# Per-row scales for whole blocks of q, and a longer planned landing for the transposed weights

## The chip, the cores and the metric

The kernel runs on one core of one Trainium2 chip. The metric is device time in microseconds of one execution, from the median of several runs. The engines are named as in the profile: PE (matmuls; PEld is its weight loads), DVE (the vector engine), ACT (the scalar engine), POOL (GpSimd) and SP (which issues the DMAs).

## What is computed

```python
B, H, S, D = 4, 8, 576, 64
scores = np.matmul(q, k.transpose(0, 1, 3, 2)) / np.sqrt(D)
kth = np.partition(scores, -32, axis=-1)[..., -32:-31]
scores = np.where(scores >= kth, scores, -1e9)
attn = np.exp(scores - scores.max(-1, keepdims=True))
attn = attn / (attn.sum(-1, keepdims=True) + 1e-9)
o = np.matmul(attn, v)
x = o.transpose(0, 2, 1, 3).reshape(B * S, H * D)
h = np.maximum(x @ w_in, 0.0)
x = h * h @ w_out
h = x @ w_in2
return (h * np.clip(h + 3.0, 0.0, 6.0) / 6.0) @ w_out2
```

Attention keeps the 32 largest scores of each row. Two layers follow, 512 to 2048 to 512 features each, over 2304 tokens.

## The kernel before

Every operand of a large matmul is split into two 16-bit parts, a high part and the rest, so that three 16-bit products stand for one 32-bit product. Before the split an operand is multiplied by a power of two, which `scale_pair` (lines 255 to 263) makes on DVE with three small operations from the exponent of a size: the scale for the operand, and its inverse for later.

A batch has 576 tokens: four blocks of 128 (whole blocks) and one of 64 (a tail). Order: 20 blocks over four batches, and in each block tiles of one head (a tail: two heads at once), 144 tiles in all. For q of a block, `q_prep` works in two halves of four heads: a load, `norm_tasks`, the split, and a DMA transpose into `qT`. `norm_tasks` (line 587) lets ACT square the operand with a running sum into `ss`, one number per partition; PE multiplies `ss` with a matrix of ones, which sums over the partitions and puts the total on each (`pnq`, line 599, in a PSUM bank of the pool `misc`); and DVE's `scale_pair` (lines 261 to 263) reads it there. For q a partition is a token, in a tail block a token too.

A tile goes through `attend`: PE multiplies q and k (`qk`, line 764, into `sp`); ACT copies the scores to S (line 770, three buffers); DVE finds the 32 largest in seven operations (lines 778 to 786) and masks the exponentials (line 801); POOL and ACT make the bias and the exponentials (lines 790, 795); ACT and POOL split the weights into `wc` (lines 806, 810, 811); SP issues a DMA transpose of `wc` into `wT` (`flip`, line 815, two buffers), and PE multiplies with the values (`av`, line 829, 14 matmuls, or 28 in a tail). When a block's tiles are through, `x_operand` makes the input of the layers (`pnx`, line 916). The layers run in groups of matmuls: `up` into `hb` (line 1075), ACT and in the second layer a gate on DVE (line 1090), a split into `ghl` on ACT and POOL, and `acc` (lines 1110 and 1118). Their scales use another `pnx` (line 1000).

The order of all instructions is made when the kernel is built. Each step is a `task` with an engine, a planned cost, a key and the tasks it needs; `Plan.run` plays a list scheduler over the engines. A task becomes ready for those that need it at its planned end plus a latency `lat`, by default one per engine (`LAT`, for SP 2.0 us). An engine takes, among its ready tasks, the one with the smallest key whose buffers are free. So PE's tasks have keys 1 for `qk`, 2 for `av`, 4 for `acc` and 5 for `up`: an `av` that is ready goes before any matmul of the layers. What comes out is one fixed list for each engine, and on the chip each engine works through its list in order and waits where an input is not there yet. The flip's task has a cost of 1.25 and the default latency:

```python
LAT = {"ACT": 0.17, "DVE": 0.14, "POOL": 0.12, "PE": 0.21, "SP": 2.0}
tw = task("SP", 1.25, (0, s), flip, deps=[tl, before[4]], alloc=["wT"])
tv = task("PE", 0.44 if len(hs) == 1 else 0.9, (2, s), av, deps=[tw, vv_task[b, hp][1], before[5]],
          alloc=["av"] if t == 0 else [])
```

Of the kernel before, what the change touches and what calls it, by code (L numbers as in the profile page):

```python
# [19 lines left out]
P = 128  # L20
# [5 lines left out]
EXP_I = float(50 << 23)  # L26
# [6 lines left out]
class Plan:  # L33
# [11 lines left out]
    def task(self, eng, cost, key, fn, deps=(), alloc=(), reads=(), writes=(), lat=None, port=False):  # L45
        t = Task(eng, cost, key, fn, tuple(alloc), lat or LAT[eng])
        t.port = port
        need = {d for d in deps if d is not None}
        for r in reads:
            need.add(self.writer.get(r))  # L50
            self.readers.setdefault(r, []).append(t)
        for r in writes:
            need.add(self.writer.get(r))
            need.update(self.readers.pop(r, ()))
            self.writer[r] = t
        need -= {None, t}
        t.left = len(need)
        for d in need:
            d.succ.append(t)
        self.tasks.append(t)  # L60
        return t

    def free(self, name, owner, *users):
        e = [len(users), name, owner]
        for u in users:
            u.rel.append(e)
# [66 lines left out]
def tile_topk_attention_moe_moe2(  # L133
# [52 lines left out]
    task, free = plan.task, plan.free  # L186
# [13 lines left out]
    def take(name, label=None):  # L200
        if name == "stg":
            return stg[plan.current.slot[name]]
        if isinstance(size[name], int):
            c = size[name] + plan.current.slot.get(name, 0)
            return scalars[:, c:c + 1]
        shape, dtype, where = size[name]
        return where.tile(shape, dtype, tag=f"{name}{plan.current.slot[name]}", name=label or name, bufs=1)
# [49 lines left out]
    def scale_pair(y_ap, inv, add, sc):  # L257

        e = scalars[:, size["e"] + nexp[0] % 4:size["e"] + nexp[0] % 4 + 1].bitcast(I32)
        nexp[0] += 1  # L260
        nc.vector.tensor_scalar(e, y_ap.bitcast(I32), EXPMASK, 1, op0=ALU.bitwise_and, op1=ALU.logical_shift_right)
        nc.vector.tensor_scalar(sc.bitcast(I32), e, -1.0, EXP_S, op0=ALU.mult, op1=ALU.add)
        nc.vector.tensor_scalar(inv.bitcast(I32), e, 1.0, add, op0=ALU.mult, op1=ALU.add)
# [49 lines left out]
    def kb(space, lo, hi):  # L313

        return [(space, n_) for n_ in range(int(lo), -int(-hi // 1))]
# [51 lines left out]
    def w_convert(i, n_, pn, par):  # L367
# [3 lines left out]
        src = kb(PLACE[i][n_][0], 4 * PLACE[i][n_][1], 4 * PLACE[i][n_][1] + 4) if PLACE[i][n_] and is64 else []  # L371
        key = CKEY[i][0] + CKEY[i][1] * n_
        low = is64 and n_ % 4 < NPOOL[i] and (i < 3 or n_ < 9)
# [210 lines left out]
    def when(kkey):  # L584
        return first[kkey[1]] + 2.0 * kkey[2] if kkey[0] == "q" else first[first_of(order, kkey[1])] + kkey[2]

    def norm_tasks(tag, src, junk, n, cost, deps, alloc, inv, kkey, reads=(), writes=()):

        box = {}

        def square():
            for a_ in alloc:
                T[a_, kkey] = take(a_)
            box["ss"] = take("ss")
            nc.scalar.activation(junk(), src(), AF.Square, accum_out=box["ss"][0:n])

        def total():
            box["pn"] = take("misc", "pn" + tag)
            nc.tensor.matmul(box["pn"][:, 0:1], ones32[0:n, :], box["ss"][0:n], start=True, stop=True)

        def scale():
            box["sc"] = take("sc" + tag)
            scale_pair(box["pn"][:, 0:1], inv(), EXP_I, box["sc"])

        t1 = task("ACT", cost, (PREP, when(kkey)), square, deps=deps, alloc=["ss", *alloc], reads=reads, writes=writes)
        t2 = task("PE", 0.2, (0, when(kkey)), total, deps=[t1], alloc=["misc"])
        t3 = task("DVE", 0.34, (0, when(kkey)), scale, deps=[t2],
                  alloc=["sc" + tag] + (["qinv"] if tag == "q" else []))
        free("ss", t1, t2)
        free("misc", t2, t3)  # L610
        return box, t1, t3

    def kv_prep(which, b, hp, deps):
# [33 lines left out]
        if which == 0:  # L647
# [5 lines left out]
            def kn5():  # L653
                return kn().rearrange("p (h c a d) -> p h c a d", h=2, c=NCH, a=2)

            bx, t1, t3 = norm_tasks("k", lambda: box["f"].rearrange("p h c d -> p (h c d)"),
                                    lambda: kn().bitcast(BF16)[:, 0:n_], P, 0.72, [l1, l2], alloc, lambda: inv, kkey,
                                    reads=rd, writes=kbn if b == 0 else [])
# [13 lines left out]
        else:  # L672
            def vv():
                return T["vv", kkey]

            bx, t1, t3 = norm_tasks("v", lambda: box["f"].rearrange("p h c d -> p (h c d)"),
                                    lambda: vv().rearrange("p a h c d -> p (a h c d)").bitcast(BF16)[:, 0:n_],
                                    P, 0.72, [l1, l2], ["vv"], lambda: inv, kkey, reads=rd)
# [8 lines left out]
    def q_prep(i, half):  # L687
# [21 lines left out]
        def qn():  # L709
            return T["kn", kkey][:, 0:16 * D].rearrange("p (h a c d) -> p h a c d", h=4, a=2, c=2)  # L710

        bx, t1, t3 = norm_tasks("q", lambda: box["f"][0:n].rearrange("p h d -> p (h d)"),
                                lambda: T["kn", kkey][0:n].bitcast(BF16)[:, 0:4 * D], n, 0.4, [l], ["kn", "qT"],
                                lambda: T.setdefault(("qinv", kkey), None) or T.__setitem__(("qinv", kkey), take("qinv"))
# [36 lines left out]
    def attend(s):  # L751
# [80 lines left out]
        before = tile_tasks[-1] if tile_tasks else [None] * 6  # L832
# [6 lines left out]
        for r in range(7):  # L839
            prev = task("DVE", 0.73 if r % 2 else 0.667, (2, s + 0.1 * r), lambda r=r: topk(r), deps=[prev],  # L840
                        alloc=["m"] if r == 0 else ["W"] if r == 1 else [])
# [7 lines left out]
                  alloc=["sums"] if t == 0 else [])  # L849
# [3 lines left out]
        th = task("ACT", 0.57, (AKEY[2], s), high, deps=[tm, before[2]], alloc=["wc"])  # L853
        tl = task("POOL", 1.38, (AKEY[3], s), low, deps=[th, before[3]])
        free("E", te, tl)
        tw = task("SP", 1.25, (0, s), flip, deps=[tl, before[4]], alloc=["wT"])
        free("wc", th, tw)
        tv = task("PE", 0.44 if len(hs) == 1 else 0.9, (2, s), av, deps=[tw, vv_task[b, hp][1], before[5]],
                  alloc=["av"] if t == 0 else [])
# [372 lines left out]
    for i, (b, j) in enumerate(order):  # L1232
        if i == first_of(order, b) and b:
            for hp in range(NHP):
                for which in range(2):
                    kv_prep(which, b, hp, late)
        if i:
            for half in range(2):
                q_prep(i, half)
        for s in range(first[i], last[i] + 1):  # L1240
            attend(s)
        x_operand(i)
# [13 lines left out]
def first_of(order, b):  # L1256
    return min(i for i, e in enumerate(order) if e[0] == b)
# [25 lines left out]
PREP = 1.5  # L1283
VKEY = 3

CKEY = ((-3.61, 0.14), (-69.99, 3.36), (-31.64, 0.91), (-0.36, 1.29))
SKEY = (0, 100, 200, 300)

# [26 lines left out]
```

## Time and profile before

| | |
|---|---|
| median of 3 runs | 1236.63 us (1236.08 to 1240.48) |
| the profiled execution's own time | 1238.58 us |
| its span, first to last instruction | 1236.8 us |
| PE, PEld, DVE busy | 1074.3, 879.4, 1058.9 us |
| ACT, POOL busy | 825.4, 663.8 us |
[...]

The durations below all come from the profiled execution. Busy shares are means over the whole span; the stretches differ, and a stretch has to be read for itself. A busy PE need not be a PE at its peak, since matmuls overlap in the records and their ends are modelled: the step from one to the next is shorter than the time of one.

### The profile page before, as it was taken

What the parts mean: (1) busy time and instruction counts of PE and PEld (TensorE: products, weight loads), DVE (VectorE), ACT (ScalarE), POOL (GpSimd) and SP (SyncE); (2) the same over time, 40 slices, a digit from 0 to 9 for tenths busy, and PEclk for the clock granted to TensorE, in tenths of its full rate; (3) what the DMA queues carried; (4) which work ended last, traced back from release to release, by engine and by line L of the source; (5) the groups of instructions that cost most, each with busy time, mean ns of one, the idle gap of its engine ahead of it and who ended that gap; (6) DMA issues with size and microseconds to landing.
All of it is one profiled execution on the core that took longest, in us unless ns stands there. A gap on an engine that the chain in (4) does not pass through costs nothing.

```text
span 1236.8 us, 36708 instructions
## 1 busy us (share of the span) xinstructions
PE 1074.3 (87%) x14856; PEld 879.4 (71%) x14856; DVE 1058.9 (86%) x2463; ACT 825.4 (67%) x1580; POOL 663.8 (54%) x969
## 2 busy tenths in 40 slices
PE   2484389878989999999899999999998999999998
PEld 2332147577679769877887888788767868978885
DVE  5999999999978999999999999999868989999011
ACT  7677588769767668666766757576866666755422
POOL 5857846458654556554545555655544555545312
PEclk9676599998999999999899999999998999999999
DMA  9989744333454233344574323435433233433100
GB/s 209 268 247 265 228 101 115 71 55 55 96 113 93 53 63 70 66 71 82 89 109 72 68 56 71 55 64 98 97 59 73 54 66 73 65 49 58 22 2 18
DMA packets 276762, 112.47 MB, mean 91 GB/s; under 512 B 257521, under 2 KB 265713, under 8 KB 276593
## 3 DMA queue, kind: packets, MB, share of 16 engines
q1 hardware_dynamic: 276592, 110.14, 43.3%
q8 instruction: 116, 1.90, 0.6%
q14 instruction: 54, 0.43, 0.1%
HBM read 48.23 MB, written 4.72 MB: 43 GB/s over the span
## 4 chain that ended last, share of the span: by engine, by line
PE 42%; DVE 15%; ACT 10%; DMA 10%; issue 5%; POOL 5%; SPq 1%; POOLq 0%; DVEq 0%; ACTq 0%
PE hb L1075 16%; PE acc L1118 9%; PE acc L1110 8%; DMA wT<-wc 8%; DVE W L783 4%; DVE m L786 4%; PE av L829 3%; PE sp L764 3%; DVE E L801 2%; DVE m L778 2%; POOL wc L810 1%; ACT E L795 1%; POOL ghl L1100 1%; ACT x L896 1%; ACT S L770 1%
## 5 line engine op out<-in xcount | busy, mean ns | idle before, releaser
L1075 PE MATMUL hb<-hl,w 128*128 128x128 f16 x6912 | 455.8, 220 | 3.7 <-ACT r L1082 2.2
L1075 PEld LDWEIGHTS <-w 128*128 128x128 f16 x6912 | 415.7, 99 | 42.8 <-issue 6.2
L786 DVE MAX8 m<-W 128x8 f32<-128x576 f32 x432 | 314.8, 747 | 0.2
L1100 POOL TENSOR_TENSOR ghl<-r,ghl 128x512 f16<-128x512 f32 x144 | 172.7, 1201 | 193.3 <-ACT ghl L1097 141.9
L1110 PE MATMUL acc<-ghl,w 128*128 128x128 f16 x3456 | 242.0, 221 | 9.9 <-POOL ghl L1100 4.2
L810 POOL TENSOR_TENSOR wc<-E,wc 128x512 f16<-128x512 f32 x144 | 167.8, 1165 | 145.2 <-ACT wc L806 117.8
L1118 PE MATMUL acc<-w,ghl 128*128 128x512 f16 x864 | 234.3, 382 | 2.8 <-POOL ghl L1100 1.5
L1110 PEld LDWEIGHTS <-w 128*128 128x128 f16 x3456 | 212.8, 99 | 29.8 <-issue 14.0
L783 DVE MATCH_REPLACE8 W<-m,W 128x576 f32<-128x576 f32 x288 | 213.3, 742 | 0.0
L795 ACT ACTIVATE E<-S,scalars,scl 128x576 f32<-128x576 f32 x144 | 124.8, 867 | 85.9 <-POOL scalars L790 65.3
L801 DVE SCALAR_TENSOR_TENSOR E<-S,m,E 128x576 f32<-128x576 f32 x144 | 137.2, 952 | 0.1
L770 ACT ACTIVATE S<-sp 128x576 f32<-128x576 f32 x144 | 92.9, 645 | 53.8 <-DVE E L801 40.9
L764 PE MATMUL sp<-kT,qT 128*128 128x288 f16 (+1 forms) x640 | 102.4, 303 | 25.0 <-ACT S L770 21.0
L829 PE MATMUL av<-vv,wT 128*128 128x64 f16 (+1 forms) x2240 | 92.7, 197 | 33.7 <-DMA wT<-wc 32.8
L829 PEld LDWEIGHTS <-wT 128*128 128x128 f16 (+1 forms) x2240 | 81.2, 103 | 56.5 <-DMA wT<-wc 46.9
L1097 ACT ACTIVATE ghl<-r 128x512 f16<-128x512 f32 x144 | 89.8, 626 | 40.9 <-PE acc L1110 21.2
L778 DVE MAX8 m<-S 128x8 f32<-128x576 f32 x144 | 107.3, 746 | 4.9 <-ACT S L770 4.9
L783 DVE MATCH_REPLACE8 W<-m,S 128x576 f32<-128x576 f32 x144 | 106.8, 741 | 0.0
L1118 PEld LDWEIGHTS <-ghl 128*128 128x128 f16 x864 | 73.8, 99 | 45.2 <-issue 3.3
L806 ACT ACTIVATE wc<-E 128x576 f16<-128x576 f32 x144 | 97.7, 679 | 4.6 <-DVE E L801 4.5
L412 POOL TENSOR_TENSOR w<-w,stg 128x512 int32<-128x512 int32 x57 | 73.0, 1294 | 35.4 <-DVE w L365 23.6
L1090 DVE SCALAR_TENSOR_TENSOR r<-r,hb 128x512 f32<-128x512 f32 x72 | 48.9, 680 | 49.6 <-ACT r L1084 49.4
(128 smaller groups left out, 1343.2 us busy)
## 6 DMA issues: line engine op xcount, KB each, us to landing
w<-in_moe_w_in_dram SPq DMA_DIRECT2D x32, 512.0 KB, 4.8
w<-in_moe_w_out_dram SPq DMA_DIRECT2D x29, 512.0 KB, 4.8
out_dram<-o SPq DMA_DIRECT2D x16, 256.0 KB, 2.4
qf<-in_q_dram SPq DMA_DIRECT2D x31, 128.0 KB, 3.1
stg<-in_k_dram SPq DMA_DIRECT2D x12, 256.0 KB, 3.2
stg<-in_v_dram SPq DMA_DIRECT2D x12, 256.0 KB, 3.1
wT<-wc SPq DMA_TRANSPOSE x144, 3.2
stg<-in_moe_w_out_dram SPq DMA_DIRECT2D x6, 256.0 KB, 3.9
```

The lines of the kernel that those rows point to most:

```text
L764: nc.tensor.matmul(dst, qT[:, 2 * ((2 * hp + hh) % 4) + a, 0:M], kflat[:, hh * SPAD + c * HALF:hh * SPAD + (c + 1) * HALF], start=a == 0, ...
L778: nc.vector.max(m[:, 0:8], T["S", s])
L783: nc.vector.match_replace(out=T["W", s], in_to_replace=m[:, 8 * c - 8:8 * c], in_values=T["S", s] if c == 1 else T["W", s], imm_value=-3.0e38)
L786: nc.vector.max(m[:, 4 * r:4 * r + 8], T["W", s])
L795: nc.scalar.activation(T["E", s], T["S", s], AF.Exp, bias=T["nb", s], scale=T["scl", ("q", i, half)][:, hp % 2:hp % 2 + 1])
L801: nc.vector.scalar_tensor_tensor(T["E", s], T["S", s], T["m", s][:, TOPK - 1:TOPK], T["E", s], op0=ALU.is_ge, op1=ALU.mult, accum_out=T["s ...
L810: nc.gpsimd.tensor_tensor(wc[:, S + TAIL:], e[:, 0:S - TAIL], wc[:, 0:S - TAIL], op=ALU.subtract)
L829: nc.tensor.matmul(out_[cols, t * D:(t + 1) * D], wT[0:kr, a, cols], vv[0:kr, vb, hh, c, :], start=n_ == 0, stop=n_ == len(prods) - 1)
L1075: nc.tensor.matmul(box["h"][:, fi * n:(fi + 1) * n], wt[2 * m][:, kk * 4 + f // 4, a, f % 4 * P:(f % 4 + 1) * P], hl[:, c, kk, 0:n], start ...
L1100: nc.gpsimd.tensor_tensor(flat(box["g"][:, 1]), flat(box["r"]), flat(box["g"][:, 0]), op=ALU.subtract)
L1110: nc.tensor.matmul(flat_[:, c * w_:c * w_ + n], wt[1][:, f, a, c * P:(c + 1) * P], gl[d], start=(f, a, d) == (0, 0, 0) and c * w_ % 512 == ...
L1118: nc.tensor.matmul(o_, gl[d][:, ch * P:ch * P + rows], wt[3][:, f, a, :], start=f == 0 and (a, d) == (0, 0), stop=f == KF - 1 and (a, d) = ...
```

## The change

Two edits. In `norm_tasks`, a q half of a whole block (`n == P`) has no sum over partitions: DVE's `scale_pair` reads `ss` itself, so each token has its own power of two, and the inverse that goes into the scores' scale differs by token as well. The task `total` on PE and its bank of `misc` fall away there; `ss` is held until DVE has read it. Tails of q, and k and v, stay as they were. In `attend`, the flip's task gets a latency of its own, `WLAT = 4.0`, in place of 2.0. That adds and removes no instruction; the planner lets `av` become ready 2.0 us later, and so gives all engines another order.

```diff
@@ -600,14 +600,17 @@
 
         def scale():
             box["sc"] = take("sc" + tag)
-            scale_pair(box["pn"][:, 0:1], inv(), EXP_I, box["sc"])
+            scale_pair(box["ss"] if rows else box["pn"][:, 0:1], inv(), EXP_I, box["sc"])
 
         t1 = task("ACT", cost, (PREP, when(kkey)), square, deps=deps, alloc=["ss", *alloc], reads=reads, writes=writes)
-        t2 = task("PE", 0.2, (0, when(kkey)), total, deps=[t1], alloc=["misc"])
+
+        rows = tag == "q" and n == P
+        t2 = t1 if rows else task("PE", 0.2, (0, when(kkey)), total, deps=[t1], alloc=["misc"])
         t3 = task("DVE", 0.34, (0, when(kkey)), scale, deps=[t2],
                   alloc=["sc" + tag] + (["qinv"] if tag == "q" else []))
-        free("ss", t1, t2)
-        free("misc", t2, t3)
+        free("ss", t1, t3 if rows else t2)
+        if not rows:
+            free("misc", t2, t3)
         return box, t1, t3
 
     def kv_prep(which, b, hp, deps):
@@ -853,7 +856,7 @@
         th = task("ACT", 0.57, (AKEY[2], s), high, deps=[tm, before[2]], alloc=["wc"])
         tl = task("POOL", 1.38, (AKEY[3], s), low, deps=[th, before[3]])
         free("E", te, tl)
-        tw = task("SP", 1.25, (0, s), flip, deps=[tl, before[4]], alloc=["wT"])
+        tw = task("SP", 1.25, (0, s), flip, deps=[tl, before[4]], alloc=["wT"], lat=WLAT)
         free("wc", th, tw)
         tv = task("PE", 0.44 if len(hs) == 1 else 0.9, (2, s), av, deps=[tw, vv_task[b, hp][1], before[5]],
                   alloc=["av"] if t == 0 else [])
@@ -1283,6 +1286,8 @@
 PREP = 1.5
 VKEY = 3
 
+WLAT = 4.0
+
 CKEY = ((-3.61, 0.14), (-69.99, 3.36), (-31.64, 0.91), (-0.36, 1.29))
 SKEY = (0, 100, 200, 300)
 
```

What moves, at two places. Line numbers after the change are larger by 3 from `scale` on. First DVE, at one half of q of a whole block of the third batch, after 76 masks. The three operations of `scale_pair` are L261 to L263, MAX and MATCH_REPLACE belong to the search for the 32 largest, and the row that writes `E,sums` is a mask. Before:

```order
L783 MATCH_REPLACE W<-m,S 128x576
L786 MAX m<-W 128x8
L261 TENSOR_SCALAR scalars<-pnq 128x1
L262 TENSOR_SCALAR scalars<-scalars 128x1
L263 TENSOR_SCALAR scalars<-scalars 128x1
L801 SCALAR_TENSOR_TENSOR E,sums<-S,m,E 128x576
L786 MAX m<-W 128x8
```

And in the changed kernel:

```order
L781 MAX m<-S 128x8
L789 MAX m<-W 128x8
L261 TENSOR_SCALAR scalars<-scalars 128x1
L262 TENSOR_SCALAR scalars<-scalars 128x1
L263 TENSOR_SCALAR scalars<-scalars 128x1
L804 SCALAR_TENSOR_TENSOR E,sums<-S,m,E 128x576
L786 MATCH_REPLACE W<-m,S 128x576
```

The three operations stand after the same number of masks; the first reads `scalars` (where `ss` lies) in place of `pnq`.

Second PE, at the 104th tile, the last of a whole block in the third batch. The first row is the last matmul of the `qk` four tiles on, the last row the first matmul of this tile's `av`; the row of `sp` above it ends the `qk` five tiles on. `ghl` and `hl` rows are the layers', pnk is the sum of a k. Before, between the two `qk` stand three matmuls of L1118, the pnk and 60 of L1075:

```order
L764 MATMUL sp<-kT,qT 64x288
L1118 LDWEIGHTS ghl
...
L599 MATMUL pnk<-scalars,ones_75 128x1
L1075 LDWEIGHTS w_88
...
L764 MATMUL sp<-kT,qT 64x288
L829 LDWEIGHTS wT
L829 MATMUL av<-vv,wT 128x64
```

And in the changed kernel (L1121 is the old L1118, L1113 the old L1110, L1078 the old L1075, L832 the old L829), where between the two `qk` stand 9 matmuls of L1121, 48 of L1113, 36 of L1078 and the `av` of the tile before:

```order
L767 MATMUL sp<-kT,qT 64x288
L1121 LDWEIGHTS ghl
...
L1113 LDWEIGHTS w_87
...
L1078 LDWEIGHTS w_88
...
L767 MATMUL sp<-kT,qT 64x288
L599 MATMUL pnq<-scalars,ones_75 128x1
L832 LDWEIGHTS wT
L832 MATMUL av<-vv,wT 128x64
```

The `av` of this tile has moved behind more work of the layers. After the last `av` of the program, PE's list has 612 matmuls of `hb`, 288 of L1110 and 108 of L1118, against 636, 288 and 114 before.

## Rows read from the trace of the kernel before

**Rows 1.** The page, part 1: busy time, share of the span, instructions.

```profile
PE 1074.3 (87%) x14856; PEld 879.4 (71%) x14856; DVE 1058.9 (86%) x2463; ACT 825.4 (67%) x1580; POOL 663.8 (54%) x969
```

**Rows 2.** Busy time of four stretches, clock, DMA share and GB/s.

```profile
0.00:20.00 20.00, 5.81 (x24) 4.30 (x24) 5.57 (x24) 12.85 (x27) 7.32 (x19) 1.00 0.87 191
20.00:150.00 130.00, 60.75 (x370) 35.32 (x371) 124.06 (x258) 86.50 (x159) 97.39 (x109) 0.67 0.89 254
150.00:1144.00 994.00, 921.65 (x13282) 769.14 (x13282) 918.42 (x2159) 692.98 (x1338) 536.49 (x816) 0.98 0.41 75
1144.00:1236.80 92.80, 86.12 (x1182) 70.61 (x1180) 10.81 (x27) 33.02 (x59) 22.58 (x25) 0.99 0.07 14
```

**Rows 3.** The page, part 4: chain of waits by line, share of the span.

```profile
PE hb L1075 16%; PE acc L1118 9%; PE acc L1110 8%; DMA wT<-wc 8%; DVE W L783 4%; DVE m L786 4%; PE av L829 3%; PE sp L764 3%; DVE E L801 2%; DVE m L778 2%; POOL wc L810 1%; ACT E L795 1%; POOL ghl L1100 1%; ACT x L896 1%; ACT S L770 1%
```

**Rows 4.** Waits of DVE, 150 to 1144 us: total us, times, longest.

```profile
DVE r L1090 <- ACT r L1084: 14.1, 15, 2.2
DVE scalars L261 <- PE pnq L599: 12.0, 11, 3.1
DVE scalars L261 <- PE pnv L599: 8.0, 8, 2.8
DVE scalars L261 <- PE pnk L599: 7.9, 8, 1.8
DVE scalars L261 <- PE pnx L1000: 6.6, 9, 1.8
DVE scalars L920 <- PE pnx L916: 5.8, 6, 1.8
```

**Rows 5.** Waits of PE in the same stretch, the two longest.

```profile
PE av L829 <- DMA wT<-wc: 32.8, 32, 2.3
PE sp L764 <- ACT S L770: 6.8, 5, 2.6
```

**Rows 6.** Instructions of tile wT: ns min/median/max of the issue, and landing.

```profile
L815 SPq DMA_TRANSPOSE wT<-wc x144: 1241/1296/2944, 45.4 to 1146.5; - x144
DMA to landing us min/median/max: 3.2/3.2/5.1
```

**Rows 7.** Groups of instructions by line: busy us, mean ns, idle before.

```profile
L599 PE MATMUL pnq<-scalars,ones 128*128 128x1 f32 (+1 forms) x80 | 15.0, 256 | 7.9 <-ACT kn L595 7.9
L599 PEld LDWEIGHTS pnq<-scalars,ones 128*128 128x128 f32 (+1 forms) x80 | 13.8, 212 | 11.4 <-ACT kn L595 5.2 <-issue 4.8 <-ACT wc L806 0.2
L261 DVE TENSOR_SCALAR scalars<-pnq 128x1 int32<-128x1 int32 x40 | 6.0, 150 | 17.6 <-PE pnq L599 17.3
L261 DVE TENSOR_SCALAR scalars<-scalars 128x1 int32<-128x1 int32 x20 | 3.1, 154 | 0.7
```

**Rows 8.** Timeline at 669 us, DVE and PE: start us, us, instruction.

```profile
668.58 0.75 DVE L786 MAX8 m<-W 128x8 f32<-128x576 f32 x1
669.96 0.16 DVE L261 TENSOR_SCALAR scalars<-pnq 128x1 int32<-128x1 int32 x1 [0.63 <-PE pnq L599]
669.59 0.34 PE L599 MATMUL pnq<-scalars,ones 128*128 128x1 f32 x2
```

**Rows 9.** The chain of waits at 909 to 922 us: start us, us.

```profile
909.18 0.65 PE acc L1118 x3
909.83 0.67 PE hb L1075 x12
922.34 0.13 PE pnq L599 x2
```

**Rows 10.** Timeline at 858 to 863 us, SP and PE.

```profile
858.38 1.29 SPq L815 DMA_TRANSPOSE wT<-wc  x1
863.19 0.58 PE L829 MATMUL av<-vv,wT 128*128 128x64 f16 x14 [1.28 <-DMA wT<-wc]
```

**Rows 11.** Waits of SP's queue for PE, whole span.

```profile
SPq L815 <- PE av L829: 7.7, 2, 7.1
```

**Rows 12.** Waits of DVE, 0 to 20 us.

```profile
DVE scalars L261 <- PE pnq L599: 5.3, 2, 4.4
```

## The prediction

> **What bounds the kernel now.** I read the busy times first, then four stretches of the span, then the waits of the two busiest engines, then the chain of waits. Over the whole span PE is busy 87% and DVE 86% [rows 1], which says only that neither is free. The stretches tell more [rows 2]. In the first 20 us every engine waits for the first loads. [...] From 150 us to the last mask at 1144 us, the long middle, PE is busy 921.7 and DVE 918.4 of 994 us: two engines at 93% and 92%, each idle some 72 to 76 us. From 1144 us on only PE matters (86.1 of 92.8 us). So the end is: the time of the last mask on DVE, plus a PE tail. DVE's idle time in the middle, 75.6 us, is what can be saved there, unless PE, with 72.4 us idle, runs full first.
>
> What ends DVE's idle time is PE, or ACT working on what PE has just made [rows 4]: the sums of q (pnq) 12.0 us, of k and v 7.9 and 8.0, of the two kinds of pnx 6.6 and 5.8, and the gate that waits for an ACT result that waits for `hb` 14.1. That is 54.4 of the 75.6 us. And what ends PE's idle time is above all one thing: the value products wait for the transposed weights, 32 times, 32.8 us, 45% of PE's idle time in the middle; the next wait is 6.8 us [rows 5]. The chain of waits agrees: the transposing transfer `wT<-wc` holds 8% of it, some 100 us, as the longest share that is no compute [rows 3].
>
> **Edit 1: q of whole blocks is scaled by its own row.** 16 of the 20 blocks are whole, with two halves each: 32 of 40 norms lose their sum over partitions. On PE that removes 64 of the 80 `pnq` matmul records and as many weight loads [rows 7]. A pair takes 0.13 us where the chain runs through it [rows 9] and at most two loads of 212 ns, so 4 to 14 us of PE's queue. DVE keeps its three small operations at the same place; only the first one's source changes. Rows show 150 ns with the PSUM source and 154 ns with an SBUF source [rows 7], so 32 x 4 ns = 0.1 us, nothing. [...]
>
> What counts is the wait. At 669.96 us DVE waited 0.63 us for a `pnq` that PE reached only at 669.59, behind other matmuls, so the hop through PE's queue was the whole wait [rows 8]. In the middle such waits are 12.0 us in 11 times [rows 4]. Two bounds: all of it goes, or none of it, if DVE then waits as long for ACT's square. The square is late in few cases: PE's own matmul waited for it twice, 7.9 us together [rows 7], none of it in the middle. So I take 9 of the 12.0 (whole blocks are four fifths of the halves). At the start pnq cost 5.3 us in two waits [rows 12]; there PE itself waited for ACT, so I take 2 (0 to 5.3).
>
> **Edit 2: the planner is told 4.0 us instead of 2.0 for the landing of a flip.** No instruction is added or gone. The list scheduler issues `av` of a tile later in PE's fixed order, and puts matmuls of the two layers before it. A flip lands 3.2 us after its issue began at best and in the median, up to 5.1 us [rows 6]; the planner counted 1.25 + 2.0 = 3.25 us, the best case without slack. One case: issued at 858.38 us, used at 863.19, PE idle 1.28 us [rows 10]. I priced PE's rows between the `qk` four tiles on and the `av` (both are set off by the same mask, which frees a score buffer for the one and feeds the other): 0.67 us for 12 matmuls of 128 columns, 0.65 for three of 512 [rows 9], some 0.5 for a `qk` or an `av`. The median over all tiles goes from about 5.1 to about 7.6 us, an estimate from the two orders: 2.5 us more cover. The longest wait was 2.3 us [rows 5]. So nearly all 32.8 us of PE's waits for flips are covered, as long as what was put before them is itself ready.
>
> How much of that reaches the end? Only what PE's lateness costs DVE: the 42.4 us of rows 4 that are not pnq. Bounds: nothing, and all 42.4. If each wait shrinks as PE's idle time does (45%), 19 us. I take a third, 14 us, as a matmul that comes forward can wait too (for S, 6.8 us now [rows 5]). The PE time of edit 1 is in this term.
>
> Against it: `av` later holds the `wT` buffer longer; there are two, SP is in order, and behind a flip that waits for an `av` stand the loads and transposes of q. Today that happens twice, 7.7 us [rows 11]. I add 3 us (0 to 15).
>
> The tail: after the last `av` PE's new order has 24 matmuls of 128 columns and 6 of 512 fewer than before; by rows 9, 2 x 0.67 + 2 x 0.65 = 2.6 us less. The cover of the transfers is gone there, but the last `av` is one instruction group.
>
> **The sum** is made against the profiled execution, 1238.6 us: -9 - 2 - 14 + 3 - 2.6 = -24.6, so 1214.0. That execution lies 2 us above the median of the runs, 1236.63. The forecast for the median is **1212 us**.
>
> **Rivals.**
> *DVE alone is the bound.* PE's waits for flips are slack that its queue makes up, and rows 4's other waits come back in other places. Then only pnq, the start and the tail are left: 1236.6 - 9 - 2 - 2.6 + 3 = 1226; with the q waits turned over to ACT as well, 1236. For it: DVE is busy as long as PE in the middle, PE's loads only 769 of 994 us [rows 2]. Against it: 54.4 of DVE's 75.6 idle microseconds are ended by PE's products. [...]
>
> *The change doesn't cover the waits.* They come from flips that are issued late (POOL waits for ACT, SP stands behind other transfers: in the case of rows 10 another transpose is in flight), and the list only moves the lateness on. Then `av` goes on waiting 20 to 30 us and the time is 1222 to 1234, around 1228. Against it: the longest wait, 2.3 us, is under the 2.5 us added.
>
> *Slower: two wT buffers.* With `av` 2.5 us later, the flip two tiles on finds no buffer; SP stops, q's transposes stop behind it, and by way of wc and E, two buffers each, ACT and DVE stop. The hold from issue to the end of `av` is now 3.2 + 0.6 us plus waits of a microsecond or two, and becomes some 7 us. Two tiles take DVE 2 x 6.9 = 13.8 us on the mean (994 us over 144 tiles), so it decides only where two masks of a neighbouring tile pair come within about 7 us. Each such wait lasts 3.9 us on the mean today (7.7 over 2 [rows 11]); if one tile in sixteen meets one, 9 x 3.9 = 35 us: 1236.6 - 24.6 + 35 = 1247. From seven tiles on the gain is gone. Against it: two such waits in the whole trace before.
>
> **Chances.** The forecast (about 1195 to 1224) 0.58; DVE alone 0.20, half of it under the line; waits not covered 0.10; slower 0.12. Half a percent is 6.2 us, about what a measurement of this kernel can tell from no change: faster is below 1230.4, slower above 1242.8. From the forecast 0.58, half of DVE alone 0.10 and most of the second rival's lower part 0.03, faster is 0.71; slower 0.12; same 0.17. The range: below, 33 of the 42.4 us instead of 14, so 1193; above, where the no-change cases end, 1238. What is left out is the slower case, and gains beyond both bounds. The likeliest case's own range is 1195 to 1224.
>
> **What would show each step.** In the profile after: `pnq` has 16 matmul records instead of 80, and DVE's waits for it in the middle are at most 3 us. PE's waits for `wT` in the middle fall from 32.8 us to under 8. DVE's waits for pnk, pnv, pnx and the gate fall from 42.4 to about 28, and DVE's idle time between 150 us and the last mask from 75.6 to about 53. The last mask ends near 1122 us, the tail stays near 90. The prediction is wrong if PE's flip waits go and DVE's idle time does not, or if PE's waits for S, `ghl` or the transposed q grow by as much, or if SP's waits for `av` grow past 15 us.

## The result and the profile after

The changed kernel takes 1207.09 us in the median (1206.4 to 1208.16), the kernel before, on the same chip, 1238.56: a ratio of 0.9747 (0.9721 to 0.9773), 31 us less. The forecast was 1212, the range 1193 to 1238.

The stretches of the kernel after, cut at its last mask (columns as in [rows 2]):

```profile
0.00:20.00 20.00, 4.85 (x24) 3.83 (x24) 6.20 (x22) 13.49 (x28) 9.73 (x22) 1.00 0.90 222
20.00:150.00 130.00, 56.21 (x354) 31.74 (x355) 123.81 (x260) 85.60 (x157) 94.19 (x105) 0.82 0.87 254
150.00:1108.00 958.00, 909.44 (x13271) 762.42 (x13270) 914.51 (x2156) 690.53 (x1339) 535.54 (x817) 0.99 0.41 77
1108.00:1203.00 95.00, 87.31 (x1148) 70.60 (x1145) 11.50 (x29) 32.08 (x57) 22.54 (x25) 0.98 0.04 13
```

In the first 150 us DVE is as busy as before (130.0 us against 129.6). The middle is 958 us instead of 994; DVE is busy 914.5 us in it, so its idle time fell from 75.6 to 43.5 us, and PE's from 72.4 to 48.6. The tail after the last mask did not get shorter: 95.0 against 92.8 us. PE's granted clock, as a share of full speed, differs in the stretch up to 150 us, 0.82 against 0.67, but the gain doesn't lie there: the 17th mask ends at 211 us in both traces. In the middle the clock is 0.99 against 0.98.

The waits of DVE in the middle of the kernel after, the first ten (total us, times, longest):

```profile
DVE r L1093 <- ACT r L1087: 10.7, 15, 2.5
DVE hl L277 <- PE acc L1121: 4.2, 3, 2.6
DVE kn L277 <- issue: 3.2, 3, 1.7
DVE scalars L923 <- PE pnx L919: 2.7, 4, 1.2
DVE scalars L261 <- ACT kn L595: 2.6, 4, 1.3
DVE vv L277 <- ACT vv L273: 2.4, 5, 0.8
DVE scalars L261 <- PE pnv L599: 1.7, 3, 0.7
DVE scalars L261 <- PE pnk L599: 1.7, 3, 0.8
DVE scalars L261 <- PE pnx L1003: 1.3, 2, 1.1
DVE scalars L261 <- PE pnq L599: 1.3, 2, 1.0
```

Against [rows 4]: pnq, which has 16 matmul records now instead of 80, 12.0 to 1.3, with 2.6 for ACT's square in its place; pnv 8.0 to 1.7, pnk 7.9 to 1.7, the two pnx 12.4 to 4.0, the gate 14.1 to 10.7. The sum of those that are not pnq is 18.1 instead of 42.4.

The waits of PE in the same stretch, the three longest:

```profile
PE sp L767 <- ACT S L773: 21.3, 20, 11.6
PE wx L536 <- ACT w L545: 2.9, 5, 1.4
PE acc L1113 <- POOL ghl L1103: 2.4, 5, 1.0
```

The waits for `wT`, 32.8 us and first in [rows 5], have left the list; what is first now is the wait for S, which grew from 6.8 to 21.3 us, 11.6 of it in one wait. SP, too, waits longer for `av`:

```profile
SPq L818 <- PE av L832: 22.5, 14, 4.9
```

That was 7.7 us in 2 times [rows 11]. In the chain of waits by line the transfer `wT<-wc`, 8% before [rows 3], is no longer among the lines shown:

```profile
PE hb L1078 16%; PE acc L1121 9%; PE acc L1113 8%; DVE W L786 4%; DVE m L789 3%; PE sp L767 2%; PE av L832 2%; DVE E L804 2%; DVE m L781 1%; ACT x L899 1%; ACT S L773 1%; ACT r L1085 1%; ACT r L1090 1%; DVE r L1093 1%; DMA kT<-kn 1%
```

So the waits of DVE and PE that were to shrink did, most of them further than forecast. Of the signs that would have made the prediction wrong one came, SP's waits for `av` over 15 us; PE's waits for S grew, but by less than half of what the waits for `wT` lost. Whether the waits that went are the cause is another question, and there the runs changed my view.

### The profile page after: what moved, and what is told of

The parts are those of the page before. It is cut to its first block, busy times and chain, and to the rows that moved or that the text cites. A ratio compares the mean times of both kernels' runs of the same rounds, so it can differ in the third digit from the quotient of the medians.

```text
span 1203.0 us, 36563 instructions
## 1 busy us (share of the span) xinstructions
PE 1057.8 (88%) x14792; PEld 868.6 (72%) x14792; DVE 1056.0 (88%) x2463; ACT 821.7 (68%) x1580; POOL 662.0 (55%) x969
## 4 chain that ended last, share of the span: by engine, by line
PE 38%; DVE 14%; ACT 7%; issue 3%; DMA 1%; POOL 1%; SPq 0%; ACTq 0%; DVEq 0%; POOLq 0%
PE hb L1078 16%; PE acc L1121 9%; PE acc L1113 8%; DVE W L786 4%; DVE m L789 3%; PE sp L767 2%; PE av L832 2%; DVE E L804 2%; DVE m L781 1%; ACT x L899 1%; ACT S L773 1%; ACT r L1085 1%; ACT r L1090 1%; DVE r L1093 1%; DMA kT<-kn 1%
## 5 line engine op out<-in xcount | busy, mean ns | idle before, releaser
L1078 PE MATMUL hb<-hl,w 128*128 128x128 f16 x6912 | 455.0, 220 | 10.5 <-POOL hl L958 2.7
L1078 PEld LDWEIGHTS <-w 128*128 128x128 f16 x6912 | 413.9, 99 | 50.8 <-issue 13.6
L1103 POOL TENSOR_TENSOR ghl<-r,ghl 128x512 f16<-128x512 f32 x144 | 173.7, 1207 | 175.1 <-ACT ghl L1100 135.5
L1113 PE MATMUL acc<-ghl,w 128*128 128x128 f16 x3456 | 237.8, 219 | 6.1 <-DVE hl L277 2.7
L1121 PE MATMUL acc<-w,ghl 128*128 128x512 f16 x864 | 231.2, 380 | 4.1 <-POOL ghl L1103 1.9
L1113 PEld LDWEIGHTS <-w 128*128 128x128 f16 x3456 | 208.1, 98 | 21.3 <-issue 8.1
L767 PE MATMUL sp<-kT,qT 128*128 128x288 f16 (+1 forms) x640 | 99.1, 296 | 40.8 <-ACT S L773 36.0
L804 DVE SCALAR_TENSOR_TENSOR E<-S,m,E 128x576 f32<-128x576 f32 x144 | 134.1, 932 | 0.0
L1121 PEld LDWEIGHTS <-ghl 128*128 128x128 f16 x864 | 74.1, 99 | 50.2 <-issue 4.8
L767 PEld LDWEIGHTS <-qT 128*128 128x128 f16 (+1 forms) x640 | 55.2, 103 | 65.7 <-issue 48.7
L1087 ACT ACTIVATE r<-hb,bias,scalars 128x512 f32<-128x512 f32 x72 | 55.6, 775 | 59.1 <-PE hb L1078 58.3
L832 PEld LDWEIGHTS <-wT 128*128 128x128 f16 (+1 forms) x2240 | 83.2, 102 | 15.4 <-issue 3.9
L832 PE MATMUL av<-vv,wT 128*128 128x64 f16 (+1 forms) x2240 | 91.1, 196 | 2.5 <-DMA wT<-wc 2.4
```

Source lines behind the costliest of these rows:

```text
L767: nc.tensor.matmul(dst, qT[:, 2 * ((2 * hp + hh) % 4) + a, 0:M], kflat[:, hh * SPAD + c * HALF:hh * SPAD + (c + 1) * HALF], start=a == 0, ...
L804: nc.vector.scalar_tensor_tensor(T["E", s], T["S", s], T["m", s][:, TOPK - 1:TOPK], T["E", s], op0=ALU.is_ge, op1=ALU.mult, accum_out=T["s ...
L832: nc.tensor.matmul(out_[cols, t * D:(t + 1) * D], wT[0:kr, a, cols], vv[0:kr, vb, hh, c, :], start=n_ == 0, stop=n_ == len(prods) - 1)
L1078: nc.tensor.matmul(box["h"][:, fi * n:(fi + 1) * n], wt[2 * m][:, kk * 4 + f // 4, a, f % 4 * P:(f % 4 + 1) * P], hl[:, c, kk, 0:n], start ...
L1103: nc.gpsimd.tensor_tensor(flat(box["g"][:, 1]), flat(box["r"]), flat(box["g"][:, 0]), op=ALU.subtract)
L1113: nc.tensor.matmul(flat_[:, c * w_:c * w_ + n], wt[1][:, f, a, c * P:(c + 1) * P], gl[d], start=(f, a, d) == (0, 0, 0) and c * w_ % 512 == ...
```

## The experiments

Theory A is the prediction's: PE's waits for the flips made PE late, PE's lateness made DVE wait. Theory B: DVE alone is the bound and the flip waits were slack. Theory C: any other order might have done it, by luck.

**e1, edit 2 alone.**

```diff
-        rows = tag == "q" and n == P
+        rows = False
```

> Edit 2 alone: q keeps its sum over partitions and PE hop, the flip's planned latency is 4.0. Theory A (waits of av for flips made PE late and PE's lateness made DVE wait): PE's waits for wT fall from 32.8 us to under 6, DVE's waits for pnk, pnv, pnx and the gate fall as in the changed kernel, DVE goes on waiting about 10 to 14 us for pnq; time 1215 to 1222. Theory B (DVE alone is the bound, flip waits were slack): PE's waits go, the time stays 1232 to 1240. Theory C (any new order would have done it): DVE's idle time falls without a link to the flip waits; the time can be anywhere.

Measured: 1211.1 us, ratio 0.9788 (0.9757 to 0.9819). The waits for `wT` are all but gone from the middle (0.8 us), pnq keeps 5.2 us, the gate falls to 4.8. Its stretch from 150 us to the last mask:

```profile
150.00:1116.00 966.00, 916.28 (x13255) 766.44 (x13255) 922.25 (x2159) 690.63 (x1338) 537.21 (x818) 0.99 0.42 77
```

DVE is idle 43.8 us in it, as little as with both edits. Theory B is out: the planned latency alone brings 27 us, 4 us more than theory A allowed. What edit 1 adds to that, 1211.1 to 1207.1 us, is less than a mere shift of the order moves (e10), so it is not shown to add anything here.

**e2, edit 1 alone.**

```diff
-WLAT = 4.0
+WLAT = 2.0
```

> Edit 1 alone: whole blocks of q are scaled per row, planned latency 2.0 as before. Theory A: DVE's waits for q fall from 17 to about 6 us, PE's waits for wT stay at 25 to 35 us, time 1224 to 1230. Theory B: the same or a little more, 1222 to 1230, and then e1 and this one don't add up. If the PE time of the sums matters beyond the wait: under 1222.

Measured: 1225.1 us, 0.9903 (0.9871 to 0.9934). The time is as theory A had it, but PE waits only 17.1 us for `wT` in the middle, where 25 to 35 were expected. DVE's waits for q are 1.2 us on PE but 15.1 us on ACT over the whole span, so most of the 17.3 us changed hands. By the medians the two edits alone would give 27 + 13 = 40 us, and the change gives 31: they don't add up.

**e3 and e4, both edits with a planned latency of 3.0 and of 6.0.**

```diff
-WLAT = 4.0
+WLAT = 3.0
```

> Both edits, planned latency 3.0 in place of 4.0. Theory A: the mean wait was 1.0 us and the longest 2.3, so 1 us more cover takes about two thirds of the waits: PE waits for wT 8 to 14 us, time 1210 to 1217. Theory C: no order along 2.0, 3.0, 4.0; the time may lie outside of what 2.0 and 4.0 give.

> Both edits, planned latency 6.0. Theory A: the waits for wT are gone at 4.0 already, so no more gain: 1204 to 1212. Rival of the two wT buffers: SP's waits for av, 22.5 us at 4.0, grow past 60 us, the loads and transposes of q behind them come late and DVE waits for them: over 1216.

Measured: 1227.9 us, 0.9921 (0.9900 to 0.9941), at 3.0; 1269.6 us, 1.0263 (1.0221 to 1.0306), at 6.0. At 3.0 PE waits only 5.8 us for `wT`, less than theory A expected, and yet nothing is gained over 2.0 (e2). That speaks against theory A as it stood: the waits can go without the time going.

At 6.0 the loss comes with the marks of the slower rival. The waits of SP for `av`, of the kernel with 6.0:

```profile
SPq L818 <- PE av L832: 184.3, 58, 7.2
```

And the waits of DVE in its middle, the first five:

```profile
DVE r L1093 <- ACT r L1087: 26.3, 20, 3.8
DVE E L804 <- ACT E L798: 13.4, 11, 6.6
DVE scalars L261 <- PE pnv L599: 13.0, 8, 4.1
DVE m L781 <- ACT S L773: 9.7, 12, 1.9
DVE scalars L261 <- PE pnq L599: 5.2, 5, 2.2
```

58 waits instead of 2 before and 14 at 4.0, and now the mask itself waits for ACT's exponentials, which it did not before. The order of PE's rows suggests why it comes so suddenly: priced as in the prediction (an estimate), the median cover in front of `av`, that is, the PE work listed before it, is 6.4 us at 3.0, 7.6 at 4.0, 8.1 at 4.5 and 17.5 at 6.0. With 6.0 the planner itself runs out of the two `wT` buffers and its own flips wait for its own `av`. That two buffers are the cause is read from waits and order; no run has a third one, so it is not shown.

**e5, only PE's list.** The kernel before; the plan is made with 2.0 as ever, and when the instructions are written out each `av` is held until 2.0 us of planned PE work have gone before it, or until something comes that needs it or the buffer that it holds. DVE, ACT, POOL and SP keep their lists row for row.

```diff
-                t.fn()
+                self.emit(t)
...
+    def emit(self, t):
...
+        if t.flip is not None:
+            self.held.append([t, 0.0])
+            return
+        self.current = t
+        t.fn()
+        if t.eng == "PE":
+            for h in self.held:
+                h[1] += t.cost
+            while self.held and self.held[0][1] >= DEFER:
+                self.flush(1)
...
```

> The kernel before with one thing changed: in PE's list alone each av stands behind 2.0 us of planned PE work more; DVE, ACT, POOL and SP keep their lists row for row. Theory A (the flip waits on PE reached DVE through PE's lateness): PE's waits for wT fall from 32.8 us to under 6 and the time to 1215 to 1225. Theory C (the gain of the new latency came from the new order of the other engines): the waits fall, the time stays at 1230 to 1240. Theory B (DVE alone is the bound): likewise 1230 to 1240.

Measured: 1240.3 us, 1.0016 (0.9991 to 1.0041): no gain at all. The cover is about the changed kernel's (7.5 us in the median, by the same estimate). The wait of PE in the whole span:

```profile
PE av L854 <- DMA wT<-wc: 2.5, 4, 1.2
```

From 32.8 us to 2.5, as was wanted. But the stretch from 150 us to the last mask, with PE, PEld, DVE, ACT and POOL busy:

```profile
150.00:1147.00 997.00, 928.52 (x13316) 776.19 (x13317) 915.69 (x2161) 692.12 (x1338) 536.36 (x817) 0.97 0.40 75
```

It is 997 us long, against 994 [rows 2]: PE is nearly as idle as before (68.5 us against 72.4), and DVE more (81.3 against 75.6). DVE's waits that answer to those of [rows 4] have not shrunk, they add up to 57.5 us instead of 54.4:

```profile
DVE r L1116 <- ACT r L1110: 14.6, 13, 3.5
DVE scalars L286 <- PE pnk L624: 11.4, 7, 4.3
DVE scalars L286 <- PE pnv L624: 10.4, 9, 2.5
DVE scalars L286 <- PE pnq L624: 9.1, 9, 2.2
DVE scalars L286 <- PE pnx L1026: 8.6, 7, 2.4
DVE scalars L946 <- PE pnx L942: 3.4, 6, 1.0
```

The waits of PE went elsewhere, among others to ACT's and SP's for `av` over the span (line 922 is the copy of the products, line 840 the flip). First ACT's, before and here:

```profile
ACT x L896 <- PE av L829: 8.3, 9, 2.2
ACT x L922 <- PE av L854: 17.3, 15, 2.9
```

And SP's here:

```profile
SPq L840 <- PE av L854: 36.0, 19, 7.5
```

SP waited 7.7 us for `av` before [rows 11]. In the old lists the copy and the next flip stand where the old `av` would have been done, and behind them stands the work of the next tile. Theory A in its simple form falls: on the old lists, PE's wait alone is worth nothing, as theories B and C had it.

**e6 and e7, q's sums left out, and both moves, on the old lists.** In e6 the planner still counts the sum; PE issues nothing for it, and DVE reads `ss`. e7 adds the move of e5.

```diff
         def total():
+            if rows:
+                return
...
-            scale_pair(box["pn"][:, 0:1], inv(), EXP_I, box["sc"])
+            scale_pair(box["ss"] if rows else box["pn"][:, 0:1], inv(), EXP_I, box["sc"])
...
```

> The kernel before with q's 32 sums of whole blocks left out of PE's list and DVE reading ss; every other row of all five lists stays where it was. Theory A: DVE's 17 us of waits for q fall to 4 to 8, time 1226 to 1232. Theory C: the 13 us of edit 1 alone were mostly the new order: 1233 to 1238.

> The two moves of the other runs together on the old order of the kernel before. Theory A: the changed kernel's time or close to it, 1204 to 1214. Theory C: at least half of the gain is missing, 1222 or more.

Measured: e6 1231.6 us, 0.9954 (0.9929 to 0.9979); e7 1230.9 us, 0.9951 (0.9929 to 0.9972). So edit 1 by itself, with nothing else moved, is worth 6 us: DVE's waits for q over the span go from 17.3 [rows 7] to 3.1 on PE and 5.5 on ACT, 8.7 us less. In e6:

```profile
DVE scalars L261 <- ACT kn L596: 5.5, 4, 3.9
DVE scalars L261 <- PE pnq L602: 3.1, 3, 2.0
```

The `av` move adds nothing to it that can be told (e7 against e6). More than half of the gain is missing on the old lists, as theory C had it for e7; e6 came out at the upper end of theory A's range.

**e8, another order without a change.** The kernel before, with the planned cost of the low half on POOL at 1.30 instead of 1.38.

> The kernel before with the planned cost of the low half of the weights on POOL at 1.30 in place of 1.38 us: nothing of the computation changes and av gets no more cover than 0.08 us, but the scheduler makes another order everywhere. Theory A: PE's waits for wT stay at 25 to 40 us, time within 10 us of before. Theory C: the time moves by as much as the change did, 20 us or more, up or down.

Measured: 1235.3 us, 0.9991 (0.9952 to 1.0030), and 31.3 us of waits for `wT` in the middle. This other order, one of many possible ones, brings nothing.

**e9, the mirror of e5.** The changed kernel's lists for DVE, ACT, POOL and SP, row for row; on PE each `av`, except a block's first, is written out as soon as a landing of 2.0 would allow it.

```diff
+                while eng == "PE" and self.avs and self.avs[0].early(now):
+                    self.current = self.avs.pop(0)
+                    self.current.fn()
...
```

> The mirror of the run with av moved: the changed kernel with its lists for DVE, ACT, POOL and SP row for row, but in PE's list each av (other than a block's first) stands as far forward as a planned landing of 2.0 us would let it; the median cover falls from 7.6 back to 5.5 us. Theory A2 (cover in front of av is worth its time only where the other lists are made for the later av, and there it is what brings the gain): PE's waits for wT come back to 20 to 35 us and the time rises to 1222 to 1238. Theory D (the gain lies in the other engines' lists, and where av stands on PE hardly matters): the waits come back, the time stays at 1204 to 1214.

Measured: 1228.1 us, 0.9922 (0.9892 to 0.9953): 21 us of the 31 are lost again. Its stretch from 150 us to the last mask, the wait of PE over the span, and the chain of waits by line (line 845 is `av`):

```profile
150.00:1131.00 981.00, 913.11 (x13272) 758.62 (x13272) 917.15 (x2158) 689.86 (x1339) 535.45 (x818) 0.99 0.40 75
```


```profile
PE av L845 <- DMA wT<-wc: 25.1, 30, 3.0
```


```profile
PE hb L1093 15%; DMA wT<-wc 9%; PE acc L1136 8%; PE acc L1128 8%; DVE W L799 5%; DVE m L802 5%; PE av L845 3%; PE sp L780 3%; DVE E L817 2%; DVE cv L375 2%; POOL wc L826 2%; DVE m L794 2%; DVE w L378 2%; PE wx L549 2%; ACT S L786 1%
```

The stretch is 981 us again instead of 958, DVE as busy as in the kernel after, so DVE's idle time is back at 64 us; the transfer is 9% of the chain, first after PE's `hb`. Here the lists of the other four engines are the same as in the changed kernel, and only the place of `av` on PE differs: with these lists, two thirds of the gain hang on that place. PE's waits for `wT` come back with it, which agrees with the cover as the cause. Theory D falls, A2 holds.

**e10 and e11, the shift of e8 on the changed kernel and on the one with 3.0.**

> The changed kernel with the planned cost of the low half on POOL at 1.30 in place of 1.38: the same work, another order, the same cover (median 7.5 us). If the gain belongs to the latency of 4.0 and not to one lucky order: 1202 to 1215. Theory C (luck of the order): anything from 1202 to 1235.

> The same shift of the planned cost on the kernel with 3.0 (median cover 6.4 us). That one measured 1228, above the 1225 of 2.0 and the 1207 of 4.0. If 1228 was that order's bad luck, this one lies between 2.0 and 4.0: 1208 to 1222. If 3.0 as such is bad: 1225 to 1232.

Measured: e10 1216.6 us, 0.9826 (0.9789 to 0.9863); e11 1227.9 us, 0.9930 (0.9886 to 0.9973). The gain at 4.0 survives another order, but is about a third smaller: 20 us against the kernel before on the same chip (1236.96), where it was 31. The time, 9.5 us above the changed kernel's, lies just outside of the forecast; so much of a time here is the order's own. At 3.0 both orders give 1228: the case "3.0 as such is bad". Why 3.0 is not half way stays open: in both, one stretch of eight masks by a change of batch takes 79 to 82 us, which takes 67 to 69 in the changed kernel, but that accounts for only 13 of the 21 us, and its cause was not tested.

**e12, both edits with a planned latency of 4.5.**

> Both edits, planned latency 4.5: the median cover of av goes from 7.6 to 8.1 us (6.4 at 3.0, 17.5 at 6.0, where the planner's own list runs out of wT buffers). Theory A2: the waits for wT are gone at 4.0, the two buffers still suffice, so 1204 to 1214 and SP's waits for av at 25 to 45 us. If the buffers begin to bind between 4.0 and 4.5: SP's waits over 45 us and the time over 1216.

Measured: 1204.9 us, 0.9720 (0.9693 to 0.9748), with SP's waits for `av` at 36.5 us in 21 times. Its interval overlaps with the changed kernel's, so it is no faster than can be told. Both forecasts of theory A2 came true, and at 4.5 no harm of the buffers shows in the time.

## Why the prediction was right, and where it was not

*What bounds the kernel.* The picture of a last mask on DVE plus a PE tail held in every run. The tail lies between 91 and 97 us throughout, and the time goes with DVE's idle time in the middle: 44 us in the changed kernel, e1 and e12 (1205 to 1211 us), 54 in e10, 59 to 73 in the runs between 1225 and 1235, 76 before, 81 in e5 and 97 at 6.0. PE's idle time goes much the same way, so this says where the time is lost and not who loses it.

*The pnq hop.* The prediction took 9 us for it in the middle and 2 at the start. In the middle it was 12.0 to 1.3, less the 2.6 that came back as ACT's square: 8.1. The 2 us of the start came to nothing: up to 150 us 5.3 us of waits for pnq became 4.9 for the square. On unchanged lists the whole was worth 6 us (e6). The bound "DVE then waits for ACT's square" was more than a bound: 5.5 us of the 17.3 came back in this way in e6, 7.5 in the kernel after, 15.1 in e2 (over the span). I looked at where PE itself waited for ACT, and that counts only the cases in which ACT was later than PE's queue.

*The cover.* That the waits for `wT` would go, and that 2.5 us of PE's rows would do it, was right (32.8 us, and none left among the waits of the middle). That the time would follow was right only for the change as a whole, and the way that was given for it was wrong. The step that failed is "How much of that reaches the end? Only what PE's lateness costs DVE", worked out on PE's list alone: the same cover on the old lists brought nothing (e5, and e7 against e6), and the new lists without it lost 21 us (e9). So the gain needs both, the later `av` and lists of the other engines that are made for it; the 32.8 us of PE's wait are not its price. The planned latency moves everything that hangs on `av`, the copy on ACT and the next flip on SP among it. That it is these copies and flips that carry the loss in e5 is read from their waits and was not tested one by one; SP's share in it is doubtful, since in e12 SP waits for `av` just as long (36.5 us) without harm.

*The size.* I took a third of the 42.4 us, 14; it was 24.3 (42.4 to 18.1). No run explains why the share was that large. The middle became 36 us shorter where I had expected 23: 32 us of it are DVE's idle time, 4 its busy time, which I had not thought of. The tail went the other way: 2.6 us less were forecast, it was 2.2 us more, with 24 and 6 matmuls fewer in the list. The records of `av`, first before, then after, with the start of the first and the last of them, show where:

```profile
L829 PE MATMUL av<-vv,wT x2240: 189/193/261, 48.8 to 1151.7; 128*128 128x64 f16 x150, 128*64 128x64 f16 x37
L832 PE MATMUL av<-vv,wT x2240: 189/193/258, 46.1 to 1118.0; 128*128 128x64 f16 x150, 128*64 128x64 f16 x37
```

From the last `av` to the end it is 85.1 us before and 85.0 after, so the missing matmuls saved nothing that shows; from the last mask to that `av` it is 7.7 us before and 10.0 after, a piece that the prediction left out. The forecast gain was 24.6 us and the measured one 31. That the forecast came within 5 us is in part luck: the term for the waits was too small, the tail and the start stood against it, and the kernel before took 2 us more here than the median that the forecast went by.

*The price of the buffers.* I added 3 us and wrote that more than 15 us of SP's waits would make the prediction wrong. They were 22.5 us, 36.5 in e12, and did no harm that the time shows; that mark was set too low, and no run shows the 3 us. At 6.0, where the kernel is 2.6% slower, the waits and the order point to the buffers; if they are the cause there, they decide from somewhere between 4.5 and 6.0, not at 4.0.

*DVE alone as the bound* was rightly the weaker rival: the planned latency brings 27 us with DVE's work unchanged (e1). In the change as a whole DVE's busy time in the middle changed by 3.9 us, its idle time by 32.1. In e1, with edit 2 alone, it is DVE's idle time that shrank, from 75.6 to 43.8 us, with its busy time at 922.3 us against 918.4 [rows 2].

## What to carry to other kernels

Where lists are fixed when the kernel is built, a planned latency sets more than one instruction's place: try some slack behind a long transfer, and let the planner move all that hangs on the result, on every engine. Try several values: here 3.0 brought nothing over 2.0, and 6.0 cost 2.6%. A wait that stands high in one engine's table is no price tag (in e5 30 of 32.8 us of it went and the time stayed, 1.0016); hold the other lists row for row and move that one instruction, both ways, before you believe it. And run a shift that means nothing: here it moved the time by up to 9.5 us, so a step that comes with a new order and is smaller than that proves little.

## What was unexpected

Removing 30 us of PE's 32.8 us of waits without touching the other lists left PE's idle time in the middle at 68.5 us (72.4 before): the wait only changed its name. And the time does not follow the planned latency evenly: 1225 us at 2.0, 1228 at 3.0, 1207 at 4.0, 1205 at 4.5, 1270 at 6.0, all with edit 1.
